# Blockwise causal attention then channel mix: the order of emission taken from a list schedule with ring buffers

## Chip, cores and metric

The kernel runs on one core of a Trainium2 chip. The metric is the time of one execution on the device in microseconds. Times are medians of runs; a profiled execution has a span (first to last instruction) and a time of its own.

## What is computed

Eight batches of eight heads, 576 positions, head size 64. Block-causal attention (blocks of 64) gives x of shape 8 x 576 x 512, and a channel mix follows on it. All inputs and the output are f32.

```python
scores = q @ k.T / sqrt(64)              # where block_i >= block_j, else -1e9
attn = softmax(scores)
x = (attn @ v) as (8, 576, 512)
x_prev = x shifted by one position, zero at the start of each batch
xk = mu_k * x + (1 - mu_k) * x_prev
xr = mu_r * x + (1 - mu_r) * x_prev
out = sigmoid(xr @ w_r) * ((relu(xk @ w_k) ** 2) @ w_v)   # w_k 512x1024, w_v 1024x512, w_r 512x512
```

## The kernel before

Attention goes batch by batch. For each pair of heads, q and k are loaded (line 84), cast to bf16 on GpSimd (98) and transposed on TensorE into PSUM (PQK, 178), and VectorE copies them out to QKT (182). The last 64 positions of all heads take a way of their own (TL, TB, lines 104 and 186). A pair's scores come in three pieces, each in two PSUM banks (PS, 208); ScalarE takes the exp into E (212), and GpSimd sets to zero the parts that the causal blocks mask (214). The piece of the last 64 positions is `score_last` (222). `av_norm` multiplies by v with a column of ones (PA, 248, 15 matmuls for a head), and VectorE divides by the sum (Rc 253, X 254). `x_transpose` turns five tiles of X (PX, 266), and ScalarE copies them into XT (282), which has positions on its free axis.

Channel mix goes in nine chunks of 512 positions, over batch borders. `mix_d` takes the difference of neighbours on GpSimd (DT, four instructions at 296) and mends the column where a batch starts (301). `mix` makes XK and XR on VectorE (304, four each). A chunk is then eight PK (315: four matmuls of 512 columns, relu on ScalarE 319, square on VectorE 320), four PR (325: four matmuls, tanh on ScalarE 328) and four PV (335: eight matmuls, then OV on VectorE 338, which multiplies by the gate, and a store on SyncE's queue 341).

The weights are loaded in f32 (138) into the buffers of q and k (`ld`, ten) and cast on VectorE (143 for w_k, 145 for w_r, 148 for w_v). Every load and store is issued on SyncE's queue.

PSUM has two pools: `pss`, two buffers of two banks each for scores, and `psm`, four buffers of one bank, which PQK, PA, PX, PK, PR and PV share.

The order is written by hand as slots: `at(slot, fn, ...)` puts the attention's steps, loads and casts at slot numbers, 13 slots to a batch, and the channel mix's PK, PR and PV are a second list, spread over fractions of slots. A loop at the end emits a step of the one list and a step of the other in turn. The framework then orders the instructions of each engine by its own priorities from this, and puts in all semaphores; so matmuls of one step can stand between those of another in the trace.

Of the kernel before, what the change touches and what calls it, by code (L numbers as in the profile page):

```python
# [9 lines left out]
FP = mybir.dt.float32  # L10
# [3 lines left out]
ALU = mybir.AluOpType  # L14


@with_exitstack
def kernel(
# [12 lines left out]
    nc = tc.nc  # L31
# [7 lines left out]
    SP_ = HP * S + D  # L39
# [7 lines left out]
    def pool(name, bufs, **kw):  # L47
        return ctx.enter_context(tc.tile_pool(name=name, bufs=bufs, **kw))

    consts = pool("consts", 1)  # L50
    ld_pool = pool("ld", 10)
    vl_pool = pool("vl", 5)
    qk_pool = pool("qk", 5)
    tl_pool = pool("tl", 2)
    tr_pool = pool("tr", 2)
    e_pool = pool("ep", 2)
    x_pool = pool("xp", 1)
    r_pool = pool("rp", 4)
    xt_pool = pool("xt", 2)
    d_pool = pool("dp", 1)  # L60
    xk_pool = pool("xk", 2)
    kr_pool = pool("kr", 3)
    k2_pool = pool("k2", 1)
    t_pool = pool("tp", 3)
    o_pool = pool("op", 3)
    ps_s = pool("pss", 2, space=PSUM)
    ps_m = pool("psm", 4, space=PSUM)
# [10 lines left out]
    LD, NB, TL, QKT = {}, {}, {}, {}  # L78

    def load_qk(b, pr):  # L80
        for n, src in enumerate((q, k)):
            LD[b, pr, n] = ld_pool.tile([P, 4, 2, D], FP, tag="ld", name="LD")
            for h in range(2):
                nc.sync.dma_start(
                    LD[b, pr, n][:, :, h],
                    src[b, 2 * pr + h, 0:512].rearrange("(t p) d -> p t d",
                                                        p=P))

    def load_tail(b):
        TL[b] = tl_pool.tile([P, H, D], FP, tag="tl", name="TL")  # L90
        for n, src in enumerate((q, k)):
            nc.sync.dma_start(TL[b][n * D:n * D + D],
                              src[b, :, 512:576].rearrange("h p d -> p h d"))

    def cast_qk(b, pr):
        NB[b, pr] = qk_pool.tile([P, 2, 4, P], BF, tag="nb", name="NB")
        for n in range(2):
            nc.gpsimd.tensor_copy(  # L98
                NB[b, pr][:, n],
                LD[b, pr, n][:, :].rearrange("p t h d -> p t (h d)"))  # L100

    def cast_tail(b):
        NB[b, 4] = tl_pool.tile([P, C], BF, tag="tb", name="TB")
        nc.gpsimd.tensor_copy(NB[b, 4],
                              TL[b][:, :].rearrange("p h d -> p (h d)"))

    VL = {}

    def load_v(b, half=None):
        hs = slice(0, H) if half is None else slice(half * HP, half * HP + HP)  # L110
        for sc in range(5):
            n = P if sc < 4 else D
            if not half:
                VL[b, sc] = vl_pool.tile([P, H, D], FP, tag="vl", name="VL")
            nc.sync.dma_start(
                VL[b, sc][0:n, hs],
                v[b, hs, sc * P:sc * P + n].rearrange("h p d -> p h d"))

    def cast_v(b, sc, half=None):
        hs = slice(0, H) if half is None else slice(half * HP, half * HP + HP)  # L120
        n = P if sc < 4 else D
        nc.gpsimd.tensor_copy(VOs[b % 2][0:n, sc, hs, 0:D],  # L122
                              VL[b, sc][0:n, hs])


# [5 lines left out]
    W = {}  # L131

    def load_w(name, i):
        src = {"k": moe_w_k, "r": moe_w_r, "v": moe_w_v}[name]
        W[name, i] = ld_pool.tile([P, C], FP, tag="ld", name="WL")
        src = src.rearrange("(cc p) (n j) -> n cc p j", p=P, j=C)
        cc, n = (i % CCn, i // CCn) if name == "k" else (i, 0)
        nc.sync.dma_start(W[name, i], src[n, cc])

    def cast_w(name, i):  # L140
        if name == "k":
            cc, n = i % CCn, i // CCn
            nc.vector.tensor_copy(WK[:, cc, n * C:n * C + C], W[name, i])
        elif name == "r":
            nc.vector.tensor_copy(WR[:, i], W[name, i])
        else:

            nc.vector.tensor_scalar_mul(WV[:, i], W[name, i], 0.5)

    for pr in range(HP):  # L150
        load_qk(0, pr)
        if pr == 0:
            load_tail(0)
        if pr == 1:
            load_v(0, 0)
    load_v(0, 1)
    nc.sync.dma_start(MUK, moe_mu_k.rearrange("(cc p) -> p cc", p=P))
    nc.sync.dma_start(MUR, moe_mu_r.rearrange("(cc p) -> p cc", p=P))
    for i in range(8):
        load_w("k", i)  # L160
# [4 lines left out]
    nc.vector.tensor_scalar_add(MUK, MUK, -1.0)  # L165
    nc.vector.tensor_scalar_add(MUR, MUR, -1.0)


    def qk_transpose(b, pr):
        if b not in QKT:  # L170
            QKT[b] = tr_pool.tile([P, 2, SP_], BF, tag="qkt", name="QKT")
            nc.vector.memset(QKT[b][:, 1, (HP * S if b else 0):], 0.0)
        pst = ps_m.tile([P, CH], FP, tag="m", name="PQK")[:, :].bitcast(BF)
        n = 8 if pr < HP else HP
        for i in range(n):
            src = (NB[b, pr][:, i // 4, i % 4] if pr < HP
                   else NB[b, HP][:, i * P:(i + 1) * P])
            nc.tensor.matmul(pst[:, i * P:(i + 1) * P], src, identb,  # L178
                             is_transpose=True, start=(i == 0),
                             stop=(i == n - 1))  # L180
        if pr < HP:
            nc.vector.tensor_copy(  # L182
                QKT[b][:, :, pr * S:pr * S + 512],
                pst.rearrange("p (n t) -> p n t", n=2))
        else:
            nc.vector.tensor_copy(
                QKT[b][:, :, 0:HP * S].rearrange(
                    "p n (a s) -> p n a s", s=S)[:, :, :, 512:S],
                pst[:, 0:HP * P].rearrange("p (a n t) -> p n a t", n=2, t=D))
# [8 lines left out]
    EP = {}  # L198

    def score(b, pr, i):  # L200
        if i == 0:
            EP[b, pr] = e_pool.tile([P, 2, 3, 512], F16, tag="e", name="E")
        E = EP[b, pr]
        PS = ps_s.tile([P, 2, 512], FP, tag="s", name="PS")
        for (col, kc, q0, n) in PIECES[i]:
            for h in range(2):
                rows = slice(h * D, h * D + D)
                nc.tensor.matmul(  # L208
                    PS[:, h, col:col + n],
                    QKT[b][rows, 1, pr * S + kc * P: pr * S + (kc + 1) * P],  # L210
                    QKT[b][rows, 0, pr * S + q0:pr * S + q0 + n], start=True, stop=True)
        nc.scalar.activation(E[:, :, i, :], PS, AF.Exp, scale=ISQ)  # L212
        for z in ZEROS[i]:
            nc.gpsimd.memset(E[D:P, :, i, z:z + D], 0.0)  # L214

    def score_last(b):
        E4 = E4s[b % 2]
        PS = ps_s.tile([P, 2, 512], FP, tag="s", name="PS4")
        for pr in range(HP):
            for h in range(2):  # L220
                rows = slice(h * D, h * D + D)
                nc.tensor.matmul(
                    PS[:, h, pr * D:pr * D + D],
                    QKT[b][rows, 1, pr * S + 512: pr * S + 640],
                    QKT[b][rows, 0, pr * S + 512:pr * S + 576], start=True, stop=True)
        nc.scalar.activation(
            E4[0:D, :, D:P].rearrange("p (a h) q -> p h a q", h=2),
            PS[0:D, :, 0:HP * D].rearrange("p h (a q) -> p h a q", q=D),
            AF.Exp, scale=ISQ)

    def stationary(b, h, kc, m):
        E = EP[b, h // 2][:, h % 2].rearrange("p i n -> p (i n)")
        if kc == 4:
            return E4s[b % 2][:, h, :]
        base = (0, 576, 1024, 1344)[kc]
        c = base + (448 if m == 4 else m * P) - kc * P
        return E[:, c:c + P]

    x_all = {}

    def av_norm(b, h):
        if h == 0:
            x_all[b] = x_pool.tile([P, 5, C], FP, tag="x", name="X")
        VO = VOs[b % 2]
        PA = ps_m.tile([P, CH], FP, tag="m", name="PA")
        for m in range(5):
            for kc in range(m + 1):
                nc.tensor.matmul(  # L248
                    PA[:, m * D1:(m + 1) * D1], stationary(b, h, kc, m),
                    VO[:, kc, h, 0:D1], start=(kc == 0), stop=(kc == m))  # L250
        Rc = r_pool.tile([P, 5], FP, tag="r", name="Rc")
# [5 lines left out]

    XT = {}

    def x_transpose(b, m):  # L260
        g0 = b * S + m * P
        rows = P if m < 4 else D
        off = 0 if m < 4 else D
# [215 lines left out]
```

## Time and profile before

| | |
|---|---|
| median of 3 runs | 334.04 us (333.43 to 334.24) |
| profiled execution, its own time | 336.05 us |
| its span | 334.2 us |
| mean granted TensorE clock | 0.949 |
| busy: TensorE, VectorE, ScalarE, GpSimd | 287.3, 204.1, 178.8, 142.0 us |
| read from and written to memory | 33.56 MB, 9.44 MB |

Busy time of an engine is the time in which at least one of its instructions runs; for TensorE the modelled end of a pipelined matmul counts in it. So a matmul's start to the next one's start says more of what it costs in a stream than its duration does. An idle time is named by what ended it: "PE PV L335 <- DVE OV L338" is TensorE standing before a PV until an OV on VectorE was done.

### The profile page before, as it was taken

What the parts mean: (1) busy time and instruction counts of PE and PEld (TensorE: products, weight loads), DVE (VectorE), ACT (ScalarE), POOL (GpSimd) and SP (SyncE); (2) the same over time, 40 slices, a digit from 0 to 9 for tenths busy, and PEclk for the clock granted to TensorE, in tenths of its full rate; (3) what the DMA queues carried; (4) which work ended last, traced back from release to release, by engine and by line L of the source; (5) the groups of instructions that cost most, each with busy time, mean ns of one, the idle gap of its engine ahead of it and who ended that gap; (6) DMA issues with size and microseconds to landing.
All of it is one profiled execution on the core that took longest, in us unless ns stands there. A gap on an engine that the chain in (4) does not pass through costs nothing. (4 is left out here: it accounts for less than half of the span.)

```text
span 334.2 us, 6717 instructions
## 1 busy us (share of the span) xinstructions
PE 287.3 (86%) x2512; PEld 150.8 (45%) x2512; DVE 204.1 (61%) x393; ACT 178.8 (54%) x257; POOL 142.0 (42%) x297
## 2 busy tenths in 40 slices
PE   2785496877978996999799969998998999979995
PEld 1454153344534552555355535554554455433442
DVE  4146693526269729681978397729682765787442
ACT  1754057424737762677357735774677485234350
POOL 4642825145683584457536663682115012250000
PEclk9999587659999997999799999999999999999999
DMA  7988974499988553393558539920100210020202
GB/s 160 225 247 205 223 236 124 116 227 239 225 205 201 116 123 83 93 229 89 145 146 188 134 86 244 207 73 33 66 2 0 75 53 2 37 89 34 94 28 97
DMA packets 122768, 43.43 MB, mean 130 GB/s; under 512 B 115568, under 2 KB 115568, under 8 KB 122736
## 3 DMA queue, kind: packets, MB, share of 16 engines
q1 hardware_dynamic: 122736, 43.01, 50.3%
q8 instruction: 19, 0.31, 0.4%
q14 instruction: 13, 0.11, 0.1%
HBM read 33.56 MB, written 9.44 MB: 129 GB/s over the span
## 5 line engine op out<-in xcount | busy, mean ns | idle before, releaser
L212 ACT ACTIVATE E<-PS 128x1024 f16<-128x1024 f32 x96 | 97.0, 1023 | 72.2 <-PE PS L208 63.0
L315 PE MATMUL PK<-XK,WK 128*128 128x512 f16 x288 | 72.5, 388 | 10.7 <-DVE XK L304 7.4
L335 PE MATMUL PV<-WV,K 128*128 128x512 f16 x288 | 72.1, 396 | 11.0 <-DVE OV L338 10.4
L214 POOL MEMSET E<- 64x128 f16 x128 | 24.0, 201 | 109.1 <-ACT E L212 106.8
L319 ACT ACTIVATE KR<-PK 128x512 f32<-128x512 f32 x72 | 43.0, 597 | 43.6 <-PE PK L315 38.8
L320 DVE TENSOR_TENSOR K<-KR 128x512 f16<-128x512 f32 x72 | 53.1, 748 | 12.2 <-ACT KR L319 12.0
L98 POOL CAST NB<-LD 128x512 bf16<-128x512 f32 x64 | 46.1, 735 | 17.7 <-DMA LD<-in_q_dram 11.2
L304 DVE SCALAR_TENSOR_TENSOR XK<-DT,MUK,XT 128x512 f16<-128x512 f32 x36 | 32.0, 932 | 28.9 <-POOL DT L301 27.7
L296 POOL TENSOR_TENSOR DT<-XT 128x512 f32<-128x512 f32 x36 | 37.6, 1071 | 23.7 <-issue 12.1
L335 PEld LDWEIGHTS <-K 128*128 128x128 f16 x288 | 28.4, 101 | 42.4 <-issue 15.4
L208 PE MATMUL PS<-QKT 64*128 64x512 bf16 (+4 forms) x320 | 41.7, 322 | 4.7 <-ACT E L212 3.7
L315 PEld LDWEIGHTS <-WK 128*128 128x128 f16 x288 | 25.6, 99 | 42.9 <-issue 12.7
L248 PE MATMUL PA<-VO,E 128*128 128x65 f16 x896 | 41.5, 200 | 0.6 <-DVE X L254 0.6
L248 PEld LDWEIGHTS <-E 128*128 128x128 f16 x896 | 35.9, 102 | 11.4 <-issue 6.0
L338 DVE SCALAR_TENSOR_TENSOR OV<-T,PV 128x512 f32<-128x512 f32 x36 | 24.5, 682 | 23.9 <-PE PV L335 21.8
L325 PE MATMUL PR<-WR,XR 128*128 128x512 f16 x144 | 38.0, 386 | 0.4 <-DVE OV L338 0.4
L178 PE MATMUL PQK<-identb,NB 128*128 128x128 bf16 x256 | 24.7, 239 | 12.3 <-POOL NB L98 12.3
L182 DVE COPY QKT<-PQK 128x1024 bf16<-128x1024 bf16 x32 | 22.0, 687 | 19.1 <-PE PQK L178 18.6
L328 ACT ACTIVATE T<-PR 128x512 f32<-128x512 f32 x36 | 21.4, 601 | 20.8 <-PE PR L325 20.8
L254 DVE TENSOR_TENSOR X<-PA,Rc 128x320 f32<-128x320 f32 x64 | 31.2, 489 | 1.6
L122 POOL CAST VO<-VL 128x512 f16<-128x512 f32 (+3 forms) x45 | 27.6, 627 | 3.6 <-PE PA L248 1.8
L282 ACT COPY XT<-PX 128x512 f32<-128x512 f32 (+1 forms) x44 | 21.6, 520 | 11.6 <-PE PX L266 11.6
(37 smaller groups left out, 183.7 us busy)
## 6 DMA issues: line engine op xcount, KB each, us to landing
out_dram<-OV SPq DMA_DIRECT2D x36, 256.0 KB, 2.1
LD<-in_q_dram SPq DMA_DIRECT2D x64, 128.0 KB, 2.9
LD<-in_k_dram SPq DMA_DIRECT2D x64, 128.0 KB, 2.9
VL<-in_v_dram SPq DMA_DIRECT2D x28, 256.0 KB, 3.8
WL<-in_moe_w_k_dram SPq DMA_DIRECT2D x8, 256.0 KB, 5.8
WL<-in_moe_w_v_dram SPq DMA_DIRECT2D x8, 256.0 KB, 2.8
VL<-in_v_dram SPq DMA_DIRECT2D x15, 128.0 KB, 3.0
TL<-in_q_dram SPq DMA_DIRECT2D x8, 128.0 KB, 3.4
```

The lines of the kernel that those rows point to most:

```text
L98: nc.gpsimd.tensor_copy(NB[b, pr][:, n], LD[b, pr, n][:, :].rearrange("p t h d -> p t (h d)"))
L208: nc.tensor.matmul(PS[:, h, col:col + n], QKT[b][rows, 1, pr * S + kc * P: pr * S + (kc + 1) * P], QKT[b][rows, 0, pr * S + q0:pr * S + q0 ...
L212: nc.scalar.activation(E[:, :, i, :], PS, AF.Exp, scale=ISQ)
L248: nc.tensor.matmul(PA[:, m * D1:(m + 1) * D1], stationary(b, h, kc, m), VO[:, kc, h, 0:D1], start=(kc == 0), stop=(kc == m))
L254: nc.vector.tensor_tensor(x_all[b][:, :, h * D:(h + 1) * D], view[:, :, 0:D], Rc[:, :].unsqueeze(2).to_broadcast([P, 5, D]), ALU.mult)
L296: nc.gpsimd.tensor_tensor(DT[:, cc], x[:, cc, 1:CH + 1], x[:, cc, 0:CH], ALU.subtract)
L304: nc.vector.scalar_tensor_tensor(XKR[c][n][:, cc], XKR[c][2][:, cc], (MUK, MUR)[n][:, cc:cc + 1], XT[c][:, cc, 1:CH + 1], ALU.mult, ALU.add)
L315: nc.tensor.matmul(ps, WK[:, cc, jc * P:(jc + 1) * P], XKR[c][0][:, cc], start=(cc == 0), stop=(cc == CCn - 1))
L319: nc.scalar.activation(KR, ps, AF.Relu)
L320: nc.vector.tensor_tensor(K2[c][:, jc], KR, KR, ALU.mult)
L325: nc.tensor.matmul(ps, XKR[c][1][:, cc, jt * P:(jt + 1) * P], WR[:, cc], start=(cc == 0), stop=(cc == CCn - 1))
L335: nc.tensor.matmul(ps, K2[c][:, jc, jt * P:(jt + 1) * P], WV[:, jc], start=(jc == 0), stop=(jc == JCn - 1))
```

## The change

The hand-written slots go. Every step becomes a task of a `Plan`, with an engine, a duration in microseconds, a rank, the tasks that it depends on, and the buffers that it takes and uses. `Plan.order` runs a list schedule: at each time, each free engine takes the task of lowest rank whose inputs are there (with a latency by engine) and whose ring has a free buffer; tasks are emitted in the order in which they start. `tc.manual_schedule()` keeps this order on every engine. SyncE's queue is planned as an engine too.

Other changes in the same diff: `psm` with four buffers becomes two rings of two, `m` for attention (PQK, PA, PX) and `mm` for channel mix (PK, PR, PV); scores keep two. Of the four subtracts of a chunk two go to VectorE, and the mending of the batch's column is split in the same way. The casts of w_r and w_v go from VectorE to ScalarE. QKT is laid out by head pair. The numbers of buffers in SBUF stay. The diff, cut to its core:

```diff
+class Plan:
+    LATENCY = {"PE": 0.12, "ACT": 0.08, "DVE": 0.08, "POOL": 0.1, "SP": 2.2}
...
+    def order(self):
+        out, now = [], 0.0
+        free = {e: 0.0 for e in self.LATENCY}
+        todo = {e: [] for e in self.LATENCY}
+        for t in self.tasks:
+            todo[t["eng"]].append(t)
+        for e in todo:
+            todo[e].sort(key=lambda t: t["rank"])
+        waiting = sum(len(x) for x in todo.values())
+        while waiting:
+            moved, nxt = False, []
+            for e, q in todo.items():
+                if free[e] > now + 1e-9:
+                    nxt.append(free[e])
+                    continue
+                for n, t in enumerate(q):
+                    at, ok = 0.0, True
+                    for d in t["deps"]:
+                        if d["end"] is None:
+                            ok = False
+                            break
+                        same = d["eng"] == e and e != "SP"
+                        at = max(at, d["end"] + (
+                            0.0 if same else self.LATENCY[d["eng"]]))
...
+                    if ok:
+                        for u in t["takes"]:
+                            k, held = self.rings[u["ring"]]
+                            if len(held) >= k:
+                                old = held[-k]
+                                if old["left"]:
+                                    ok = False
+                                    break
+                                at = max(at, old["free"])
+                    if not ok:
+                        continue
+                    if at > now + 1e-9:
+                        nxt.append(at)
+                        continue
+                    t["start"], t["end"] = now, now + t["dur"]
+                    free[e] = t["end"]
...
+                    out.append(t)
...
-    ps_s = pool("pss", 2, space=PSUM)
-    ps_m = pool("psm", 4, space=PSUM)
+    RINGS = {"ld": 10, "vl": 5, "nb": 5, "tl": 2, "tb": 2, "qkt": 2, "e": 2,
+             "x": 1, "r": 4, "xt": 2, "d": 1, "xk": 2, "xr": 2, "kr": 3,
+             "k2": 1, "t": 3, "o": 3, "s": 2, "m": 2, "mm": 2, "vo": 2, "el": 2}
+    plan = Plan(RINGS)
...
+    ctx.enter_context(tc.manual_schedule())
...
+    LAG = 3
+    SOON = -1000
+    def step(b, n=0):
+        return b * NP_ + n - (40 if b == 0 else 0)
...
+    def add_w(name, n, rank):
...
+                if name == "k":
+                    nc.vector.tensor_copy(WK[:, cc, half * C:half * C + C], w)
+                elif name == "r":
+                    nc.scalar.copy(WR[:, i], w)
+                else:
+                    nc.scalar.activation(WV[:, i], w, AF.Copy, scale=0.5)
...
+    def add_qkt(b, pr, rank):
+        m = plan.buf("m")
...
+        t = on("PE", 0.47 if pr < HP else 0.25, rank, fn, deps,
...
+        evac["qkt", b, pr] = on(
+            "DVE", 0.7 if pr < HP else 0.45, SOON, ev,
...
+    def add_av(b, h, rank, halves):
+        m = plan.buf("m")
...
+        t = on("PE", 0.47, rank, fn, deps,
...
+        evac["x", b, h] = on(
+            "DVE", 0.73, rank, norm,
...
+    def add_mix(c, rank):
+        MIXR = rank - 6
...
+            eng = "DVE" if cc < 2 else "POOL"
...
+                (nc.vector if eng == "DVE" else nc.gpsimd).tensor_tensor(
+                    tiles["d", c][:, cc], x[:, cc, 1:CH + 1], x[:, cc, 0:CH],
+                    ALU.subtract)
+            sub.append(on(eng, 0.68 if eng == "DVE" else 1.07, MIXR, fn,
...
+                dep = [sub[cc]] + ([fixed[cc // 2]] if fixed else [])
+                mixed[c, n, cc] = on(
+                    "DVE", 0.76, MIXR + 3 * n, fn,
...
+    def add_pk(c, jc, rank):
+        m, kr = plan.buf("mm"), plan.buf("kr")
...
+        t = on("PE", 0.87, rank, fn,
...
+        t = on("ACT", 0.56, SOON, relu, [t], takes=[kr], uses=[m])
...
+        act["k2", c, jc] = on(
+            "DVE", 0.73, SOON, sq,
...
+        t = on("DVE", 0.69, SOON, ov, [t, act["t", c, jt]], takes=[o],
+               uses=[m, tiles["tbf", c, jt]])
...
+    add_loads(0, [-90, -88, -86, -85], [-87, -84], 2)
...
+    add_w("k", 8, -26)
     for b in range(B):
+        if b + 1 < B:
+            r = b * NP_
+            add_loads(b + 1, [r - 8, r - 7, r - 6, r - 5], [r - 4])
+        if b == 0:
+            add_w("r", 4, -3)
+            add_w("v", 8, -2)
+        r = step(b, -3)
+        for pr in (0, HP, 1, 2, 3):
+            add_qkt(b, pr, r if pr == HP else r + pr)
+        r = step(b)
...
+        for h in range(H):
+            add_av(b, h, r + 6 + 3 * (h // 2) + h % 2, 2 if b == 0 else 1)
+        for mt in range(5):
+            add_xt(b, mt, r + NP_ + 3)
         for c in ((b,) if b < B - 1 else (b, b + 1)):
+            add_mix(c, step(b, NP_ + 3.5 + c - b))
     for c in range(NCH):
+        first = step(c + 1, 6) + LAG
+        us = [(add_pk, jc) for jc in range(JCn)]
+        us += [(add_pr, 0), (add_pr, 1), (add_pv, 0), (add_pr, 2),
+               (add_pv, 1), (add_pr, 3), (add_pv, 2), (add_pv, 3)]
+        for i, (f, j) in enumerate(us):
+            f(c, j, first + i * NP_ / len(us))
+    for t in plan.order():
+        t["fn"]()
```

## Rows read from the trace of the kernel before

**Rows 1.** The page: busy us (share of the span) and instructions of each engine

```profile
PE 287.3 (86%) x2512; PEld 150.8 (45%) x2512; DVE 204.1 (61%) x393; ACT 178.8 (54%) x257; POOL 142.0 (42%) x297
```

**Rows 2.** Stretches: length; busy of PE, PEld, DVE, ACT, POOL; granted clock, DMA share, GB/s

```profile
0.00:31.00 31.00, 20.49 (x224) 12.79 (x224) 13.43 (x40) 14.78 (x17) 13.37 (x43) 1.00 0.87 214
31.00:60.00 29.00, 18.51 (x130) 9.05 (x131) 16.37 (x23) 12.54 (x19) 16.38 (x27) 0.73 0.67 180
...
110.00:296.00 186.00, 173.68 (x1601) 91.94 (x1601) 123.98 (x231) 113.70 (x167) 84.95 (x173) 0.98 0.39 99
...
0.00:50.00 50.00, 32.16 (x281) 18.00 (x282) 26.89 (x60) 20.82 (x27) 24.36 (x57) 0.90 0.86 216
```

**Rows 3.** Waits of TensorE, 110 to 296 us: total, times, longest

```profile
PE PV L335 <- DVE OV L338: 10.4, 5, 2.7
```

**Rows 4.** Timeline of TensorE: start, us, line, tiles, count, idle before

```profile
129.14 3.25 PE L335 MATMUL PV<-WV,K 128*128 128x512 f16 x8 [2.67 <-DVE OV L338]
```

**Rows 5.** Timeline of VectorE ahead of that PV

```profile
124.38 4.11 DVE L304 SCALAR_TENSOR_TENSOR XK<-DT,MUK,XT 128x512 f16<-128x512 f32 x4 [3.76 <-POOL DT L301]
128.41 0.67 DVE L338 SCALAR_TENSOR_TENSOR OV<-T,PV 128x512 f32<-128x512 f32 x1
```

**Rows 6.** Waits of TensorE, 31 to 110 us

```profile
PE PK L315 <- DVE XK L304: 7.4, 3, 6.6
PE PQK L178 <- POOL NB L98: 6.3, 8, 1.5
```

**Rows 7.** Timeline of TensorE where it runs without a gap

```profile
117.51 0.66 PE L266 MATMUL PX<-identf,X 128*128 128x128 f32 x4
118.01 1.89 PE L335 MATMUL PV<-WV,K 128*128 128x512 f16 x8
...
138.20 0.39 PE L208 MATMUL PS<-QKT 64*128 64x320 bf16 x4
138.52 0.62 PE L178 MATMUL PQK<-identb,NB 128*128 128x128 bf16 x8
138.98 0.59 PE L248 MATMUL PA<-VO,E 128*128 128x65 f16 x14
...
170.64 0.58 PE L248 MATMUL PA<-VO,E 128*128 128x65 f16 x14
...
171.09 1.89 PE L315 MATMUL PK<-XK,WK 128*128 128x512 f16 x8
...
313.11 7.07 PE L315 MATMUL PK<-XK,WK 128*128 128x512 f16 x32
320.01 1.89 PE L325 MATMUL PR<-WR,XR 128*128 128x512 f16 x8
321.74 1.89 PE L335 MATMUL PV<-WV,K 128*128 128x512 f16 x8
...
326.92 3.62 PE L335 MATMUL PV<-WV,K 128*128 128x512 f16 x16
```

**Rows 8.** The page: bytes of the whole execution

```profile
HBM read 33.56 MB, written 9.44 MB: 129 GB/s over the span
```

**Rows 9.** Timeline of SyncE's queue: v weights, then batch 2's first q

```profile
43.64 19.11 SPq L138 DMA_DIRECT2D WL<-in_moe_w_v_dram  x8
63.69 0.93 SPq L84 DMA_DIRECT2D LD<-in_q_dram  x2
```

**Rows 10.** Groups of instructions: busy us, mean ns of one | idle before, releasers

```profile
L296 POOL TENSOR_TENSOR DT<-XT 128x512 f32<-128x512 f32 x36 | 37.6, 1071 | 23.7 <-issue 12.1 <-DVE XR L304 6.8 <-ACT XT L282 2.7
L304 DVE SCALAR_TENSOR_TENSOR XK<-DT,MUK,XT 128x512 f16<-128x512 f32 x36 | 32.0, 932 | 28.9 <-POOL DT L301 27.7 <-POOL DT L296 1.2
L304 DVE SCALAR_TENSOR_TENSOR XR<-DT,MUR,XT 128x512 f16<-128x512 f32 x36 | 26.8, 762 | 0.0
L148 DVE TENSOR_SCALAR WV<-WL 128x512 f16<-128x512 f32 x8 | 2.8, 418 | 0.0
```

**Rows 11.** Timeline of ScalarE in the last stretch

```profile
315.03 0.60 ACT L319 ACTIVATE KR<-PK 128x512 f32<-128x512 f32 x1 [0.27 <-PE PK L315]
```

More of the change, by code (lines that the diff above doesn't have):

```diff
@@ L164 @@
         nc.vector.memset(E4s[i], 0.0)
[L165 to L174, printed above, removed]
-        for i in range(n):
[L176 to L180, printed above, removed]
+    NP_ = 13
@@ new lines, with load, fn, on @@
+    LAG = 3
+    SOON = -1000
+    def step(b, n=0):
+        return b * NP_ + n - (40 if b == 0 else 0)
+    tiles = {}
+    def load(dst_key, make, jobs, rank, dur, deps=(), takes=(), uses=()):
+        def fn():
+            if make is not None:
+                tiles[dst_key] = make()
+            for dst, src in jobs(tiles[dst_key]):
+                nc.sync.dma_start(dst, src)
+        return plan.add("SP", dur, rank, fn, deps, takes, uses)
+    def on(eng, dur, rank, fn, deps, takes=(), uses=()):
+        return plan.add(eng, dur, rank, fn, deps, takes, uses)
@@ L197, with add_score @@
     ZEROS = [[0], [64], [0, 320]]
-    EP = {}
-    def score(b, pr, i):
+    ready = {}
+    def add_score(b, pr, i, rank):
+        s = plan.buf("s")
         if i == 0:
[L202 to L229, printed above, removed]
+            tiles["ebuf", b, pr] = plan.buf("e")
@@ L242, in av_norm @@
         if h == 0:
[L243 to L251, printed above, removed]
-        view = PA[:, 0:5 * D1].rearrange("p (m e) -> p m e", e=D1)
@@ new lines, in add_av, with xt_tile @@
+        evac["x", b, h] = on(
+            "DVE", 0.73, rank, norm,
+            [t] + ([evac["x", b, 0]] if h else []),
+            takes=[plan.buf("r")], uses=[m, xbuf])
+    xtbuf = [plan.buf("xt") for _ in range(NCH)]
+    xt_parts = {c: [] for c in range(NCH)}
+    def xt_tile(c):
+        if ("xt", c) not in tiles:
+            tiles["xt", c] = new("xt", [P, CCn, CH + 1], FP)
+            if c == 0:
+                nc.vector.memset(tiles["xt", c][:, :, 0:1], 0.0)
+        return tiles["xt", c]
@@ L271, in x_transpose, with add_xt @@
+    def add_xt(b, mt, rank):
+        m = plan.buf("m")
+        g0 = b * S + mt * P
+        rows, off = (P, 0) if mt < 4 else (D, D)
+        parts = []
         done = 0
         while done < rows:
[L273 to L281 removed]
@@ L344 @@
[L344 to L358 removed]
+            c, at = divmod(g0 + done, CH)
+            n = min(rows - done, CH - at)
+            parts.append((c, at, n, done, not xt_parts[c]))
@@ new lines, in add_xt, with fn @@
+            if not xt_parts[c]:
+                xt_parts[c].append(None)
+            done += n
+        def fn():
+            for p in parts:
+                xt_tile(p[0])
+            px = tiles["px", b, mt] = new("m", [P, CH], FP)
+            for cc in range(CCn):
+                nc.tensor.matmul(
+                    px[:, cc * P:(cc + 1) * P],
+                    tiles["x", b][:, mt, cc * P:(cc + 1) * P], identf,
+                    is_transpose=True, start=(cc == 0), stop=(cc == CCn - 1))
@@ new lines, in add_xt, with cp @@
+        t = on("PE", 0.46, rank, fn, [evac["x", b, h] for h in range(H)],
+               takes=[m] + [xtbuf[p[0]] for p in parts if p[4]],
+               uses=[tiles["xbuf", b]]
+               + [xtbuf[p[0]] for p in parts if not p[4]])
+        for c, at, n, done, first in parts:
+            def cp(c=c, at=at, n=n, done=done):
+                nc.scalar.copy(
+                    xt_tile(c)[:, :, 1 + at:1 + at + n],
+                    tiles["px", b, mt][:, :].rearrange(
+                        "p (c t) -> p c t", t=P)[
+                            :, :, off + done:off + done + n])
+            xt_parts[c].append(on("ACT", 0.15 + n * CCn / 1200, rank, cp, [t],
+                                  uses=[m, xtbuf[c]]))
```

624 lines of the change are left out of this document (364 added, 260 removed).

## The prediction

> **What bounds the kernel now.** I read the page's busy line first, then the span cut into stretches, then TensorE's waits in each stretch, then its timeline where it never waits. TensorE is the busiest engine, 287.3 of 334.2 us, with VectorE next at 204.1 [rows 1].
>
> The stretches put sizes to this [rows 2]. Up to 31 us there are 224 matmuls, which is exactly one batch of attention (36 transposes in, 48 for scores, 120 for attention times values, 20 transposes out). From 31 to 60 us only 130 follow, at a mean granted clock of 0.73, between the two levels 1.2 and 2.4 GHz. From 110 to 296 us TensorE is busy 173.68 of 186 us.
>
> From 110 to 296 us one cause makes nearly all of the idle time: five waits of PV for the OV of VectorE, 10.4 us [rows 3]. One of them shows how: PV starts at 129.14 after 2.67 us of nothing [rows 4], because OV, which frees a PSUM buffer, stood on VectorE's queue behind four XK in a row that take 4.11 us from 124.38 [rows 5]. The eight matmuls of that PV then take 3.25 us, where the same group takes 1.73 in a later stretch [rows 4, 7]: the clock had fallen after the hole. From 31 to 110 us the waits are others: 7.4 us for the first XK and 6.3 for casts of q and k [rows 6].
>
> **How much work TensorE really has.** Busy time counts drains and slow-clock time, so I count tasks and take the start-to-start time of each where TensorE runs without a gap [rows 7]. Eight PK take 320.01 - 313.11 = 6.90 us, so 0.86 each; two PR 1.73, so 0.86; a PV (eight matmuls) 1.73, by which two last longer than one (3.62 against 1.89); a score task 0.32; a PQK 0.46; one head of PA 0.45; a PX 0.50. The small transposes and the small scores are estimated at 0.22 each, about half a PQK. A batch of attention is 12 x 0.32 + 8 x 0.45 + 4 x 0.46 + 5 x 0.50 + 2 x 0.22 = 12.2 us. A chunk of channel mix is 8 x 0.86 + 4 x 0.86 + 4 x 1.73 = 17.3 us. All of it: 8 x 12.2 + 9 x 17.3 = 253 us. The profiled span is thus 81 us above the work, and TensorE is the engine to fill.
>
> By 60 us the kernel before has done the 12.2 us of batch 0, eight PK (6.9) and about 98 small matmuls of batch 1 (98 / 224 x 12.2 = 5.3): 24.4 us. The other 229 us take until 330.5, the end of the last PV [rows 7]: 85% efficiency. In 110 to 296 us alone it is better: 10.8 us idle and 2% of the clock gone [rows 2, 3] leave about 92%.
>
> **Loads.** The order of the first loads stays as it is: batch 0, the k weights, batch 1, then r and v weights. The core reads 33.56 MB [rows 8], of which the weights are 20 tiles of 256 KB, 5.24 MB; a batch is (33.56 - 5.24) / 8 = 3.54 MB. Two batches and all weights are 12.3 MB. In the first 50 us the queues moved 216 GB/s at a share of 0.86 [rows 2], so they need 57 us whatever the order. That bounds the start, and the change can't move it. What it can move is what follows: before, the eight v-weight loads sit in SyncE's queue from 43.64 us for 19.11 us, since they wait for load buffers that the r-weight casts free, and those stand on VectorE behind a normalization that waits; the loads of batch 2 follow only at 63.69 [rows 9]. In the new kernel these casts are on ScalarE, and each load is issued where the plan has its buffer free, so batch 2 follows directly. This removes some 8 us of an idle queue. It hides behind TensorE's backlog unless TensorE runs dry at 67 us, as it does now.
>
> **The first 57 us.** After batch 0 the chain is transposes out, copies, subtract, mix, PK. The four subtracts are serial on GpSimd at 1.07 each [rows 10] and all four come before any XK, with batch 1's casts behind them. Now two go to VectorE, each XK waits for its own subtract only (and a boundary fix), and the casts of batch 1 have lower ranks and go first. I expect PK 2 to 4 us earlier and batch 1's transposes and scores in the hole of 6.6 us. By 57 us the new kernel can have done batch 0 (12.2), the PK and PR of chunk 0 (10.4) and four fifths of batch 1 (9.8): 32.4, taken as 33. The ends are 25 (as before) and 38 (all of batch 1 and part of PV).
>
> **From 57 us on.** The plan takes apart the blocks that cause the waits: squares, OV and the QKT copies carry a rank that always goes first, so OV waits behind at most one mix step (0.93) and not four (4.11). Of the five waits of about 2 us, one step's remainder stays, at most 0.93 each: from 10.4 to under 4.7 us, and with them goes the clock's 2%. The waits for casts (6.3) should go too, since loads and casts run about a batch ahead. Against this stands what is added on VectorE: 18 subtracts, bounded by 0.76 and 0.93 (the two-input mix steps on the same shapes [rows 10]; I take 0.8, near the one beside an idle GpSimd, since its load falls): 14.4 us; eight half fixes and wider zero fills, under 3 us; minus 12 weight casts of 0.42 [rows 10], 5 us. VectorE goes from 204 to about 217 us. Less about 30 by 57 us, that is 187 in 234, 80%: a queue, no bound. ScalarE gains these 12 casts, by its nearest row, a relu of 0.60 on the same shape [rows 11], 7 us on 179, covered by its idle time except in the start, where exps and relus compete with them. GpSimd loses 18 x 1.07 = 19 us. Other operations keep their count and their shape; QKT's new layout moves bytes inside the tile only.
>
> The rings: attention's transposes, heads and transposes out now have two banks and channel mix two, where four were shared. For channel mix alone two do: in the last stretch relu starts 0.9 us after its PK's start and takes 0.60 [rows 11], so a bank is free 1.5 us after, before the third PK at 1.73 us. In attention a bank is held for 0.45, an eviction of about 0.7 (as OV's 0.67 [rows 5]) and the queue in front; the plan puts other work between, at its own durations (PK 0.87, score 0.44, PA 0.47), which are at or above the measured ones, so engines should arrive early rather than late. I take an efficiency of 0.94 from 57 us on: above the 0.92 of the best long stretch now, below the 0.98 that removing all five waits would give. The ends are 0.88 (VectorE's queue costs more than the old waits) and 0.97.
>
> **Sum.** 57 + (253 - 33) / 0.94 + 3.7 (from the last PV's end to the span's end, unchanged) = 294.7 us of span. The median before (334.04) equals the span (334.2) within 0.2, so I forecast 295. The ends of the terms: 57 + (253 - 38) / 0.97 + 3.7 = 282, and 57 + (253 - 25) / 0.88 + 3.7 = 320.
>
> **Rivals.**
> 1. *The start gains nothing.* PK comes no earlier, since ScalarE now has exps, relus and twelve casts together, and batch 1 waits for it. Then 24.4 us are done by 60 and the rest runs at 0.94: 60 + 229 / 0.94 + 3.7 = 307. For it: in 31 to 60 us ScalarE was busy only 12.54 [rows 2], waiting most of the time, so it speaks rather against. Chance 0.15.
> 2. *VectorE becomes the bound.* Its 80% with one more engine in its chain (subtract, fix, XK, all there) turns the old waits into many short ones, efficiency 0.88: 57 + 220 / 0.88 + 3.7 = 311. For it: VectorE is already the engine that every late wait names [rows 3]. Against: its idle third. Chance 0.17.
> 3. *Slower: the split rings.* Of 18 attention tasks per batch (5 transposes in, 8 heads, 5 out), 144 in all, each holds one of only two banks. TensorE takes its queue in order, and now the order is frozen; what is queued behind a waiting head is also the PK that VectorE and ScalarE live from. If each waits 0.27 us for its bank, the 39 us of gain are gone; at 0.35 us it is 295 + 144 x 0.35 = 345. For it: with four banks shared PV already waited for OV [rows 3, 4]. Against: the order was made with these rings, so a bank is late only by what the real engines differ from the plan. Chance 0.07. The Trainium skill (Perfetto Trace Analysis, Optimization Strategy) says that the same gap repeating on the engine that should be full can mean too little SBUF or PSUM for the next tile; the old trace agrees with 10.4 us of waits for a bank, and by that rule two banks would give this rival's time. No run here shows it yet.
> 4. *No change.* The old order was near what this one does, and the loads decide: then efficiency after 60 us stays at 0.85 and the time at 334. The 10.4 and 7.4 us of waits with a named cause in the order speak against it. Chance 0.03.
>
> The forecast has 0.58. Faster by over 0.3% (about what a measurement of this kernel can tell from no change): forecast and rivals 1 and 2, 0.90. Within 0.3%: 0.03. Slower: 0.07. The range 282 to 320 takes in rivals 1 and 2 and leaves out 3, 4 and an even better filling; about 0.85.
>
> **What would show it.** Right: no wait of PV for OV over 1 us, VectorE's XK in single steps between squares, first PK before 35 us, v weights issued by 52 us and batch 2 behind them, granted clock at 2.4 GHz from about 60 us, the chain of waits at the end all TensorE, VectorE near 217 us. Wrong: TensorE waiting for PA's or PQK's bank hundreds of times (rival 3), or for XK in mid-kernel (rival 2), or fewer than 400 matmuls by 57 us, where batch 0, 48 matmuls of chunk 0 and four fifths of batch 1 make 450 (rival 1).

## The result

The changed kernel takes 312.39 us (median of 4, 311.82 to 314.44) against 334.14 in the same session: a ratio of 0.936, with a 95% interval of 0.9315 to 0.9407. It is 21.7 us faster where I forecast 39. The profiled execution took 312.19 us with a span of 310.4. Two of the five executions of the first experiment's kernel ran about 5 us longer at a lower granted clock, so its time below is that of the other three.

| us | before | after |
|---|---|---|
| span | 334.2 | 310.4 |
| mean granted TensorE clock | 0.949 | 0.969 |
| busy TensorE | 287.3 | 274.2 |
| busy VectorE | 204.1 | 225.2 |
| busy ScalarE | 178.8 | 186.0 |
| busy GpSimd | 142.0 | 124.8 |

In the new kernel the buffers have other names: `t_m` and `t_mm` are the PSUM banks of attention and of channel mix, `t_d` is the difference (line 523), `t_xk` and `t_xr` the mixes (549), `t_k` the square (590), `t_o` the output (636), `t_x` the normalized head (444), `t_nb` a q or k cast (212), `t_xt` the transposed x (492). Its page and its stretches, which answer to [rows 1, 2] (length; busy of PE, PEld, DVE, ACT, POOL; clock, DMA share, GB/s):

```profile
PE 274.2 (88%) x2512; PEld 150.5 (48%) x2512; DVE 225.2 (73%) x407; ACT 186.0 (60%) x269; POOL 124.8 (40%) x279
```

```profile
0.00:31.00 31.00, 16.91 (x208) 10.70 (x209) 13.90 (x39) 13.36 (x14) 13.49 (x44) 0.96 0.90 204
31.00:60.00 29.00, 25.47 (x205) 14.44 (x205) 21.19 (x36) 21.91 (x36) 15.48 (x28) 0.81 1.02 256
60.00:110.00 50.00, 43.56 (x460) 26.11 (x459) 36.24 (x63) 33.99 (x48) 35.96 (x72) 0.97 1.05 223
110.00:270.00 160.00, 153.88 (x1487) 84.13 (x1485) 129.54 (x235) 102.43 (x148) 56.88 (x135) 1.00 0.41 101
270.00:310.40 40.40, 34.40 (x156) 15.15 (x155) 24.31 (x36) 14.33 (x24) 3.04 (x2) 0.98 0.16 59
```

Up to 31 us TensorE now does less (208 matmuls where it did 224), from 31 to 60 us much more (205 for 130), with the DMA engines at a share of 1.02 where they had 0.67. From 110 to 270 us it is busy 96% of the time at a granted clock of 1.00. What it still waits for, in the whole span (total, times, longest):

```profile
PE t_m L303 <- POOL t_nb L212: 6.6, 5, 4.9
PE t_mm L626 <- DVE t_o L636: 4.8, 5, 1.6
PE t_m L482 <- DVE t_x L444: 3.9, 1, 3.9
PE t_s L358 <- ACT t_e L368: 3.2, 5, 1.0
PE t_m L426 <- DVE t_x L444: 2.9, 2, 2.6
PE t_mm L573 <- DVE t_xk L549: 2.2, 1, 2.2
```

PV's wait for OV is down from 10.4 to 4.8 us [rows 3] but not gone. New is a single wait of 3.9 us of the transposes out for a normalized head; the first row's 4.9 us is the wait for the first load.

### The profile page after: what moved, and what is told of

Its sections match the earlier page's. It is cut to its first block, busy times and chain, and to the rows that moved or that the text cites. A ratio compares the mean times of both kernels' runs of the same rounds, so it can differ in the third digit from the quotient of the medians.

```text
span 310.4 us, 6718 instructions
## 1 busy us (share of the span) xinstructions
PE 274.2 (88%) x2512; PEld 150.5 (48%) x2512; DVE 225.2 (73%) x407; ACT 186.0 (60%) x269; POOL 124.8 (40%) x279
## 5 line engine op out<-in xcount | busy, mean ns | idle before, releaser
L368 ACT ACTIVATE t_e<-t_s 128x1024 f16<-128x1024 f32 x96 | 95.7, 1026 | 48.6 <-PE t_s L358 48.3
L573 PE MATMUL t_mm<-t_xk,WK 128*128 128x512 f16 x288 | 70.2, 383 | 4.1 <-DVE t_xk L549 2.2
L626 PE MATMUL t_mm<-WV,t_k 128*128 128x512 f16 x288 | 67.3, 379 | 5.1 <-DVE t_o L636 4.8
L590 DVE TENSOR_TENSOR t_k<-t_kr 128x512 f16<-128x512 f32 x72 | 53.5, 756 | 11.8 <-ACT t_kr L584 11.6
L584 ACT ACTIVATE t_kr<-t_mm 128x512 f32<-128x512 f32 x72 | 43.1, 599 | 27.0 <-PE t_mm L573 24.8
L212 POOL CAST t_nb<-t_ld 128x512 bf16<-128x512 f32 x64 | 43.0, 680 | 36.8 <-DMA t_ld<-in_q_dram 19.6
L426 PEld LDWEIGHTS <-t_e 128*128 128x128 f16 x896 | 34.7, 99 | 17.4 <-issue 5.8
L358 PE MATMUL t_s<-t_qkt 64*128 64x512 bf16 (+4 forms) x320 | 37.6, 313 | 5.4 <-ACT t_e L368 3.2
L426 PE MATMUL t_m<-VO,t_e 128*128 128x65 f16 x896 | 38.9, 196 | 3.8 <-DVE t_x L444 2.9
L603 PE MATMUL t_mm<-WR,t_xr 128*128 128x512 f16 x144 | 36.2, 380 | 0.0
L523 POOL TENSOR_TENSOR t_d<-t_xt 128x512 f32<-128x512 f32 x18 | 23.8, 1336 | 18.0 <-issue 9.8
L523 DVE TENSOR_TENSOR t_d<-t_xt 128x512 f32<-128x512 f32 x18 | 19.6, 1119 | 15.4 <-ACT t_xt L492 15.3
```

What stands on the lines that cost most here:

```text
L212: nc.gpsimd.tensor_copy(tiles["nb", b, pr][:, n], tiles[key][:, :].rearrange("p t h d -> p t (h d)"))
L358: nc.tensor.matmul(PS[:, h, col:col + n], qkt[rows, pr, 1, kc * P:kc * P + P], qkt[rows, pr, 0, q0:q0 + n], start=True, stop=True)
L368: nc.scalar.activation(tiles["e", b, pr][:, :, i, :], tiles["ps", b, pr, i], AF.Exp, scale=ISQ)
L426: nc.tensor.matmul(PA[:, mt * D1:(mt + 1) * D1], stationary(b, h, kc, mt), VOs[b % 2][:, kc, h, 0:D1], start=(kc == 0), stop=(kc == mt))
L523: (nc.vector if eng == "DVE" else nc.gpsimd).tensor_tensor(tiles["d", c][:, cc], x[:, cc, 1:CH + 1], x[:, cc, 0:CH], ALU.subtract)
L573: nc.tensor.matmul(ps, WK[:, cc, jc * P:(jc + 1) * P], tiles["xk", c][:, cc], start=(cc == 0), stop=(cc == CCn - 1))
```

## The experiments

My theory: the gain is the order of the list schedule, kept on every engine; the split rings cost nothing and the moves between engines little. Rivals: any kept order would do; the moves make the gain; the rings matter. All ratios are to the kernel before, on the same chip.

**The planned order, not kept.**

```diff
-    ctx.enter_context(tc.manual_schedule())
```

> The changed kernel with the line that keeps the planned order taken out: the framework orders each engine's instructions itself, from the planned emission. Theory (the gain of 21.7 us, 334.1 to 312.4, is the list schedule's order and needs to be kept on every engine): 318 to 330 us, since the framework moves single matmuls and VectorE steps between each other again. Rival (what helps is the new engines of the casts and subtracts, or the loads; the order's details do nothing): 309 to 315 us.

Measured 349.47 us (349.34 to 350.62), ratio 1.047 (1.042 to 1.052): some 15 us slower than the kernel before, and further than my theory's end of 330. All other parts of the change are in this kernel, QKT's new layout too, which was not run by itself. So none of them gives the 21.7 us without the order, and the same emission handed to the framework is worse than the hand slots were.

**The hand order, kept.** The same line added to the kernel before.

> The kernel before with its hand-written slots, and the emission order kept on every engine. Theory (the list schedule's order is the gain): no gain, 334 us or more, up to 350, since slots without the framework's reordering put waiting steps in front. Rival (keeping any order is enough): under 325 us.

Measured 360.61 us, ratio 1.079 (1.075 to 1.083). Keeping an order is no gain by itself. Up to 14 us of this are one accident of the hand order, shown by VectorE's and TensorE's waits:

```profile
DVE MUK L166 <- DMA MUK<-in_moe_mu_k_dram: 16.1, 1, 16.1
PE PS L209 <- DVE QKT L183: 13.9, 1, 13.9
```

The small step on MUK was emitted first and waits for its load, with the first QKT copy queued behind it. Without it, by an estimate of 360.6 - 13.9, the time would still be about 347, above the kernel before; no run shows it.

**The moves between engines alone**, in the kernel before:

```diff
-            nc.gpsimd.tensor_tensor(DT[:, cc], x[:, cc, 1:CH + 1],
-                                    x[:, cc, 0:CH], ALU.subtract)
+            (nc.vector if cc < 2 else nc.gpsimd).tensor_tensor(
+                DT[:, cc], x[:, cc, 1:CH + 1], x[:, cc, 0:CH], ALU.subtract)
...
-            nc.vector.tensor_copy(WR[:, i], W[name, i])
+            nc.scalar.copy(WR[:, i], W[name, i])
...
```

> The kernel before with only the moves between engines: two of four subtracts and half of each fix on VectorE, the casts of w_r and w_v on ScalarE; order by hand slots. Theory (the order is the gain): 328 to 336 us; the r and v weights come earlier, since their casts no longer stand behind a waiting normalization, worth up to 6 us, and VectorE loses some of it. Rival (the moves make most of the gain): 312 to 322 us.

Measured 330.08 us, ratio 0.987 (0.984 to 0.991): 4 us, as the theory had it. Alone they are a small part.

**One ring of four banks in the changed kernel.**

```diff
-             "k2": 1, "t": 3, "o": 3, "s": 2, "m": 2, "mm": 2, "vo": 2, "el": 2}
+             "k2": 1, "t": 3, "o": 3, "s": 2, "m": 4, "vo": 2, "el": 2}
...
-        m, kr = plan.buf("mm"), plan.buf("kr")
+        m, kr = plan.buf("m"), plan.buf("kr")
...
```

> The changed kernel with one ring of four PSUM banks for attention and channel mix in place of two rings of two; the plan runs with that ring. Theory (two banks each are enough, since TensorE waits for a bank in few places: 4.8 us for OV in five waits and 2.6 us for one X): within 2 us of the changed kernel, 310 to 315. Rival (the split rings hold back part of the gain): 300 to 309 us. The other rival (the split is part of the gain, since four shared banks can all fill with one kind): over 316 us.

Measured 306.19 us, ratio 0.917 (0.913 to 0.920), 6 us better than the changed kernel: my theory fell, the rival that the split holds back part of the gain is right (the plan is made again with this ring, so the order differs too). From 110 to 270 us TensorE's busy time goes from 153.88 to 157.86 of 160 us, and the wait for OV is nearly gone there (first fence: the changed kernel; second: one ring):

```profile
PE t_mm L626 <- DVE t_o L636: 4.8, 5, 1.6
PE t_mm L573 <- ACT t_kr L584: 0.7, 1, 0.7
```

```profile
PE t_s L358 <- ACT t_e L368: 1.0, 1, 1.0
PE t_m L626 <- DVE t_o L636: 0.7, 2, 0.4
```

**The split alone**, in the kernel before: `psm` with two banks for PQK, PA and PX, a second pool with two for PK, PR and PV.

> The kernel before with its four shared PSUM banks split in two and two, as in the change; hand order. Theory (the split by itself costs, as one ring of four in the changed kernel gave 306 where two of two gave 312): 337 to 345 us. Rival (the 6 us came from another plan, not from the banks): 333 to 336 us.

Measured 341.35 us, ratio 1.023 (1.019 to 1.026): 7.6 us slower. PV's waits for OV between 110 and 300 us rise from 10.4 us in five [rows 3] to 14.1 in seven. That is 3.7 of the 7.6 us; where the rest goes is not traced:

```profile
PE PV L336 <- DVE OV L339: 14.1, 7, 2.7
```

With either order the split costs 6 to 8 us. The Trainium skill (Perfetto Trace Analysis, Optimization Strategy) says that the same gap repeating on the engine that should be full can mean too little PSUM; these two runs agree, with 14.1 us where four shared banks have 10.4, and 4.8 us where one ring has 0.7. The gap is in PV, whose bank waits longest for VectorE and which with the split can't take one of attention's.

**All subtracts and fixes on GpSimd again**, in the changed kernel:

```diff
-            eng = "DVE" if cc < 2 else "POOL"
+            eng = "POOL"
...
-                for half, eng in enumerate(("DVE", "POOL")):
+                for half, eng in enumerate(("POOL", "POOL")):
```

> The changed kernel with all four subtracts of a chunk and the whole fix on GpSimd again (the plan reorders with that). Theory (the split is near neutral: it takes about 24 us off VectorE, by the 19.6 us of its subtracts and the 5.2 us of its fixes, but gives back the shorter chain to XK): 310 to 316 us. Rival A (the shorter chain from XT to PK is part of the gain): 317 to 324 us. Rival B (VectorE at 225 us busy is what holds the changed kernel at 310, and subtracts on two engines slow each other, 1119 and 1336 ns where 1071 alone): 303 to 309 us.

Measured 325.41 us, ratio 0.974 (0.969 to 0.979): 13 us lost, just past rival A's end. VectorE falls from 225.2 to 203.1 us of busy time and the kernel is slower, so what VectorE's load gave back was less than what the longer chain cost. Between 31 and 60 us TensorE does 162 matmuls (205 with the split subtracts), and at the end nothing covers the chain. GpSimd, VectorE and TensorE there:

```profile
274.95 4.03 POOL L523 TENSOR_TENSOR t_d<-t_xt 128x512 f32<-128x512 f32 x4 [4.84 <-issue]
```

```profile
279.14 2.74 DVE L549 SCALAR_TENSOR_TENSOR t_xk<-t_d,MUK,t_xt 128x512 f16<-128x512 f32 x4 [4.12 <-POOL t_d L536]
```

```profile
279.94 0.38 PE L573 MATMUL t_mm<-t_xk,WK 128*128 128x512 f16 x1 [2.81 <-DVE t_xk L549]
281.27 8.16 PE L573 MATMUL t_mm<-t_xk,WK 128*128 128x512 f16 x30 [0.17 <-DVE t_xk L549]
```

Four serial subtracts, then XK, then PK: 4.12 us of idle VectorE and 2.81 of TensorE, and then 30 PK matmuls in 8.16 us, where 32 took 7.07 [rows 7]; from 282 to 284 us the granted clock was 0.50. With the matmuls counted by line and priced as in the forecast, this kernel is 6.7 us of work behind the changed one by 110 us, and from 270 us to the last PV it loses 6.5 us more. The plan differs too, so the 13 us are of the move with its own order. In the hand order all moves together were worth 4 us. So the part of my theory that the moves do little fell as well: the plan without this one gains 8 us (333.70 to 325.41), and this one with the plan the other 13.

**All subtracts and fixes on VectorE.** The base of this run and the next is the kernel with one ring and the casts of w_k on ScalarE (304.89 us, below).

> The kernel with one ring and the w_k casts on ScalarE (304.9 us), with all four subtracts and the whole fix on VectorE. Theory (a subtract takes 1.1 to 1.2 us on VectorE only since GpSimd runs its own beside it): the mean of one falls to 0.70 to 0.85 us, VectorE's busy time stays within 10 us of 220 to 225, and the time within 3 us of 304.9. Rival (a subtract of two f32 tiles costs VectorE 1.1 us by itself): mean over 1.05 us, VectorE over 235 us busy, 308 to 316 us.

Measured 308.28 us, ratio 0.923 (0.918 to 0.928). Groups of the changed kernel, then of this one (busy us, mean ns of one | idle before), and for each VectorE's subtracts alone (shortest, median and longest in ns):

```profile
L523 POOL TENSOR_TENSOR t_d<-t_xt 128x512 f32<-128x512 f32 x18 | 23.8, 1336 | 18.0 <-issue 9.8 <-ACT t_kr L584 7.7 <-ACT t_xt L492 0.4
L523 DVE TENSOR_TENSOR t_d<-t_xt 128x512 f32<-128x512 f32 x18 | 19.6, 1119 | 15.4 <-ACT t_xt L492 15.3
L536 DVE COPY t_d<-t_xt 128x2 f32<-128x2 f32 x8 | 5.2, 653 | 0.3
L523 DVE TENSOR_TENSOR t_d<-t_xt x18: 678/734/2877, 34.6 to 272.7; 128x512 f32<-128x512 f32 x18
```

```profile
L523 DVE TENSOR_TENSOR t_d<-t_xt 128x512 f32<-128x512 f32 x36 | 25.0, 752 | 13.9 <-ACT t_xt L492 13.8
L536 DVE COPY t_d<-t_xt 128x2 f32<-128x2 f32 x16 | 2.7, 209 | 0.0
L523 DVE TENSOR_TENSOR t_d<-t_xt x36: 678/685/1097, 33.9 to 277.9; 128x512 f32<-128x512 f32 x36
```

The time is 0.4 us past the theory's band, where the rival's begins; of the cause the theory holds: the mean subtract on VectorE takes 752 ns when GpSimd runs none beside it, and 1119 when it does; GpSimd's take 1336 beside VectorE and 1071 to 1083 where all four are its own. The 1119 is a mean of unlike ones: of the 18, ten took 0.68 to 0.78 us, seven 1.1 to 1.5, and one, which stood beside two of GpSimd's, 2.88. One of the two engines waits while the other runs. The fix of two columns falls from 653 to 209 ns. VectorE's busy time is 219.3 us with twice the subtracts. The Trainium skill (SBUF — State Buffer, Who interferes with whom) says that a VectorE instruction with two SBUF inputs contends with a GpSimd instruction that reads SBUF, for ports that one of them holds at a time; the trace agrees, with the 2.88 us. The time did not fall by it; it is 3.4 us above the base.

**Both half fixes on GpSimd**, same base.

> The kernel with one ring and the w_k casts on ScalarE (304.9 us), with both halves of the fix on GpSimd; subtracts stay two and two. Theory (the half fix of 0.57 to 0.65 us on VectorE, 4.5 to 5.2 us in all, is off the path most of the time): 304 to 307 us. Rival (each batch's chain from subtract to XK ends through it): 300 to 303 us, or over 309 us if GpSimd's queue makes it later.

Measured 307.34 us, ratio 0.919 (0.914 to 0.924), where the base has 0.911 (0.909 to 0.914): slightly slower than the base and 0.3 us past the theory's band. Taking the fix off VectorE gains nothing.

**A later arrival of loads in the plan**: `"SP": 2.2` becomes `5.0`, in the changed kernel.

> The changed kernel with the plan's latency of loads at 5.0 us in place of 2.2; the trace shows 3.4 to 5.8 from issue to landing. Theory (the plan's loads come too early on paper, so the casts of w_k stand in front of batch 0's last normalizations on VectorE and TensorE waits 3.9 us for X, and first PK is at 43.05 us): first PK before 40 us, the long wait for X gone, 306 to 310 us. Rival (loads set the start, so an earlier PK only waits later): 311 to 314 us.

Measured 314.44 us, ratio 0.943 (0.940 to 0.946). The time is the rival's or just past it, but not its reason: the wait for X is still 3.8 us and the first PK stands at 42.41 us. The casts still came first. So this run didn't take the suspect away; the next does.

**The casts of w_k on ScalarE**, in the kernel with one ring:

```diff
-                    nc.vector.tensor_copy(WK[:, cc, half * C:half * C + C], w)
+                    nc.scalar.copy(WK[:, cc, half * C:half * C + C], w)
```

> The kernel with one ring of four banks (306.2 us), and the casts of w_k on ScalarE, which stands idle from 24 to 31 us, in place of VectorE, where they stood between batch 0's last normalizations and waited for their loads. Theory (these casts, waiting on VectorE's queue, are why TensorE has nothing for 4 us at 26 us and the first PK is late): the wait for X or for VectorE's step before XT goes from 4 to under 1 us, first PK before 39 us, 302 to 304.5 us. Rival (the loads set the start; an earlier PK is given back by 60 us): 305 to 307 us.

Measured 304.89 us, ratio 0.911 (0.909 to 0.914). VectorE in the changed kernel, and TensorE with the casts on VectorE (changed kernel) and on ScalarE:

```profile
25.45 0.43 DVE L275 CAST WK<-t_ld 128x512 f16<-128x512 f32 x1 [0.55 <-DMA t_ld<-in_moe_w_k_dram]
27.56 0.43 DVE L275 CAST WK<-t_ld 128x512 f16<-128x512 f32 x1 [1.68 <-DMA t_ld<-in_moe_w_k_dram]
28.23 0.43 DVE L275 CAST WK<-t_ld 128x512 f16<-128x512 f32 x1 [0.25 <-DMA t_ld<-in_moe_w_k_dram]
28.57 0.18 DVE L443 RECIPROCAL t_r<-t_m 128x5 f32<-128x5 f32 x1
```

```profile
29.43 0.87 PE L482 MATMUL t_m<-identf,t_x 128*128 128x128 f32 x3 [3.94 <-DVE t_x L444]
43.05 1.89 PE L573 MATMUL t_mm<-t_xk,WK 128*128 128x512 f16 x4
```

```profile
26.99 1.64 PE L482 MATMUL t_m<-identf,t_x 128*128 128x128 f32 x13 [0.63 <-DVE t_xt L459]
39.80 1.91 PE L573 MATMUL t_m<-t_xk,WK 128*128 128x512 f16 x4
```

The mechanism is as the theory says: VectorE stood before casts whose loads had not landed, with batch 0's last normalizations queued behind, and without them the wait of 4 us (3.94 in the changed kernel, 4.1 with one ring) is 0.63. The first PK is at 39.80 (41.45 with one ring alone), not before 39 as the theory said. The time gained is 1.3 us against 306.19, and the two intervals touch (0.9085 to 0.9137 and 0.9134 to 0.9200): most of the earlier start is given back, as the rival had it. By 60 us TensorE has done 410 matmuls, and 412 with one ring alone. In absolute terms this is the fastest kernel of the study.

**The casts of w_r and w_v on VectorE**, in the changed kernel.

> The changed kernel with the casts of w_r and w_v on VectorE again, 12 of 0.4 us in place of 0.6 on ScalarE. Theory (with the list schedule no cast stands behind a waiting normalization for long, so where they run does nothing): 311 to 315 us. Rival (the place of the casts gives the earlier v weights and part of the gain): 317 us or more.

Measured 314.69 us, ratio 0.944 (0.940 to 0.947), inside the theory's band; the intervals with the changed kernel touch.

**Measured durations in the plan**, one ring.

> The kernel with one ring of four banks (306.2 us), and the plan's durations set to what the changed kernel's trace shows: score 0.33 (was 0.44), PX 0.50 (0.46), PA 0.45, small transposes and scores 0.22, exp 0.95, subtract 1.12 on VectorE and 1.34 on GpSimd (0.68 and 1.07), fix 0.65 and 0.3 (0.2), mix 0.83 (0.76), q and k casts 0.68. Theory (the order is what counts, engines run it at their own speed, and a few tenths in the plan do little): 303 to 309 us. Rival (the waits that are left come from the plan's wrong durations, the subtracts' above all): 296 to 302 us.

Measured 309.33 us, ratio 0.924 (0.921 to 0.927): 0.3 us past the far end of the theory's band, 3 us worse than the round guesses, and nowhere near the rival's 302. A truer plan is no better here; I can't say why it is worse.

## Why the prediction was right, and where it missed

It said 295, within 282 to 320, faster with 0.90; measured 312.4, faster. Direction and range held; the point is 17 us low. Of its signs of being right only the loads came in full: PV still waits for OV up to 1.6 us, the mixes stand in pairs, and the first PK is not before 35 us. By its own steps:

**What bounds it.** Right. TensorE is the engine to fill, and filling it is the gain.

**Span for time.** I took the span as the time, since median and span before agreed. The profiled execution's time was 1.85 us above its span (336.05 and 334.2), and after it is again 1.8 (312.19 and 310.4). So some 2 of the 17 us are this; the sum of 294.7 is to be held against 310.4.

**The first 57 us.** The loads did as said: the v weights are issued from 45.10 to 51.27 us, where they stood until 62.75 before [rows 9], and batch 2 follows:

```profile
45.10 6.17 SPq L185 DMA_DIRECT2D t_ld<-in_moe_w_v_dram  x8
51.47 0.93 SPq L185 DMA_DIRECT2D t_ld<-in_q_dram  x2
```

The step "PK 2 to 4 us earlier" failed: the first PK is at 43.05 us, where it was at 37.49. The w_k casts in front of the normalizations are shown as a cause (39.80 without them and with one ring). A second is in the plan: its PK is one task that needs all four XK. Before, the first matmul of PK ran after the first XK, and the next PK from 40.53; now the first XK starts at 38.35, 2 us later than before, but PK waits for the fourth. TensorE before and VectorE after:

```profile
37.49 0.61 PE L315 MATMUL PK<-XK,WK 128*128 128x512 f16 x1 [6.58 <-DVE XK L304]
40.53 1.86 PE L315 MATMUL PK<-XK,WK 128*128 128x512 f16 x4 [0.43 <-DVE XK L304]
```

```profile
38.35 3.07 DVE L549 SCALAR_TENSOR_TENSOR t_xk<-t_d,MUK,t_xt 128x512 f16<-128x512 f32 x3
41.95 1.11 DVE L549 SCALAR_TENSOR_TENSOR t_xk<-t_d,MUK,t_xt 128x512 f16<-128x512 f32 x1
```

Batch 1's attention in that hole did come as said. By 57 us there are 398 matmuls, not 450. By 60 us there are 412: batch 0 (224), 32 PK and 12 PR (9.5 us), six of a PV's eight (1.3 us) and 138 small ones (138 / 224 x 12.2 = 7.5): 30.5 us of work. My 33 by 57, carried on at 0.94, would be 35.8: 5 us short.

**From 57 us on.** The efficiency is the term that was mis-sized. The last PV ends at 305.5 us:

```profile
301.88 3.61 PE L626 MATMUL t_mm<-WV,t_k 128*128 128x512 f16 x16
```

What was left at 60 us, 253 - 30.5 = 222.5 us, took 245.5: 0.91, not 0.94, and that is 9 us. After the last PV come 4.9 us, not the unchanged 3.7: 1 us. With the 2 us of span for time and the 5 of the start these make up the 17; all err to the same side, so none hides another.

Where the 9 us are lost shows when the matmuls of each stretch are counted by line and priced as in the forecast. From 60 to 110 us it is 40.7 us of work in 50, or 0.81 (before 32.4, or 0.65); from 110 to 270 us it is 149.6 in 160, or 0.94 (before, from 110 to 296, 163.5 in 186, or 0.88). So the long stretch came out as forecast, and some 7 of the 9 us were lost before 110 us, for which the sum had no term of its own. The "about 92%" from which the forecast rose to 0.94 was another measure: it was worked out from idle time and clock, with 10.8 us idle where [rows 2] give 186 - 173.68 = 12.3, and by the counted work that the sum uses the old stretch had 0.88.

Idle time after 60 us is 13.7 us: 6.4 from 60 to 110, 6.1 from 110 to 270 and 1.1 after. Slower clock is some 2. The other 7 of the 23 us above the counted work are a remainder, busy time beyond my start-to-start times, which no run takes apart.

The longest wait from 60 to 110 us is one of attention for a bank. VectorE, then TensorE:

```profile
76.93 2.50 DVE L549 SCALAR_TENSOR_TENSOR t_xk<-t_d,MUK,t_xt 128x512 f16<-128x512 f32 x2
79.36 2.54 DVE L549 SCALAR_TENSOR_TENSOR t_xr<-t_d,MUR,t_xt 128x512 f16<-128x512 f32 x2
```

```profile
82.58 0.58 PE L426 MATMUL t_m<-VO,t_e 128*128 128x65 f16 x14 [2.62 <-DVE t_x L444]
```

Four mix steps stood in front of a head's normalization, which is not among the steps whose rank always goes first. With one ring of four banks such waits fall from 2.9 us to 0.9.

Three more steps behind the 0.94 failed in the trace, though the long stretch reached it:

- "For channel mix alone two do" was worked out for PK, whose bank is free after 1.5 us. PV's is not: OV waits on VectorE behind the mixes. Shown by one ring of four, 6.2 us faster; counted as above it does 154.1 us of work from 110 to 270 us, or 0.96.
- "OV waits behind at most one mix step": the trace has mixes in pairs (two XK took 2.71 us from 109.86), dearer where they stand beside GpSimd's subtracts and casts (2.71 us for that pair, 1.40 for the XR pair at 115.78), and five waits up to 1.6 us. The last of three in a row here took 1.09 us, with OV behind it and PV behind OV. The rank puts OV first only where OV is ready at the time that the plan has; the frozen order then holds where it comes later.

```profile
109.86 2.71 DVE L549 SCALAR_TENSOR_TENSOR t_xk<-t_d,MUK,t_xt 128x512 f16<-128x512 f32 x2
112.50 1.09 DVE L549 SCALAR_TENSOR_TENSOR t_xr<-t_d,MUR,t_xt 128x512 f16<-128x512 f32 x1
113.51 0.67 DVE L636 SCALAR_TENSOR_TENSOR t_o<-t_t,t_mm 128x512 f32<-128x512 f32 x1
```

```profile
114.24 1.89 PE L626 MATMUL t_mm<-WV,t_k 128*128 128x512 f16 x8 [1.60 <-DVE t_o L636]
```

- VectorE's added work: I bounded a subtract by 0.76 and 0.93 and took 0.8; it is 1.12 on average, outside both bounds, since the two engines that share the subtracts slow each other. With fixes of 0.65 VectorE came to 225 us, not 217. With all of them on VectorE the slowing is mostly gone, and the time is no shorter.

**The clock.** At full speed from 60 us on, said the forecast; it is 0.97 from 60 to 110, 1.00 from 110 to 270 and 0.98 after. Nearly right.

**The rivals.** Rival 1 (no gain at the start) has its sign, fewer than 400 matmuls by 57 us (398), and a later PK, but neither its reason nor its result: the casts that ScalarE took over cost nothing there (314.69 with them on VectorE), and 30.5 us of work are done by 60 us against 24.4. For rival 2 (VectorE the bound) nothing speaks: 22 us less on VectorE, by a longer chain, made the kernel 13 us slower, and 5 us less of fixes gained nothing. Rival 3 named the right mechanism at the wrong size and in the wrong ring: the split costs 6 to 8 us, in channel mix's PV more than in attention. Rival 4 is out.

**What was underrated.** I gave the split of the subtracts no term of its own beyond an earlier first PK. In the planned order it is worth 13 us, at the start and at the end, where no other work covers the chain from XT to PK; without it the time, 325, would have been outside the range. And the framework's own order of the same emission is some 15 us slower than the kernel before: without the line that keeps the order nothing of the gain is left.

## What to carry to other kernels

A good order pays only together with what keeps it on every engine, and keeping a poor one makes it worse: judge the two as one. Count PSUM banks at the engine that evicts last, not at the fastest evictor, and split a shared ring only if a run shows that it helps. Before the last stretch and before the first, look for the chain that nothing covers and shorten it, even if that loads a busier engine.

## What the runs showed of the hardware

A subtract of two f32 tiles of 128 x 512 takes 0.68 to 0.69 us on VectorE and 1.03 to 1.04 on GpSimd where nothing of the other engine stands beside it. Side by side the means are 1119 and 1336 ns, and one engine waits while the other runs. So sharing gains little throughput. Four of them end 4.0 us after the first one's start on GpSimd alone (274.95, above), 3.0 us shared two and two (259.68 to 262.71), and 2.5 us on VectorE alone; the first two lines are of the changed kernel:

```profile
259.68 2.14 DVE L523 TENSOR_TENSOR t_d<-t_xt 128x512 f32<-128x512 f32 x2
259.78 2.93 POOL L523 TENSOR_TENSOR t_d<-t_xt 128x512 f32<-128x512 f32 x2 [7.37 <-issue]
```

```profile
259.54 2.50 DVE L523 TENSOR_TENSOR t_d<-t_xt 128x512 f32<-128x512 f32 x4
```

A copy of two columns on VectorE takes 653 ns on average beside GpSimd's subtracts and 209 without them.
